# Attention, two MoE layers: where the loads, poolings and scatters of batches 4 to 7 stand in a hand-written order

## The chip, the cores and the metric
The kernel runs on one core of a Trainium2 chip. The core has five engines that work in parallel, each through its own instructions in program order: PE (matmul), DVE (VectorE), ACT (ScalarE), POOL (GpSimd) and SP, which here only issues DMAs. ACT and POOL issue DMAs too. The metric is the time of one execution in microseconds, on the device; the changed kernel is timed against this one.

## The reference
Three layers follow each other, in float32. Attention has 8 batches, 8 heads, 576 tokens and a head size of 64; keys and values are first averaged over groups of 8 tokens, so that each head has 72 of them.

```
k_p = k.reshape(B, H, 72, 8, D).mean(axis=3)          # v_p alike
attn = softmax(q @ k_p.T / sqrt(D));  x = attn @ v_p    # x: 4608 tokens x 512
e = argmax(x @ w_gate + modality_bias[modality_id])     # layer 1: one of 8 experts per token
x = gate_w * (relu(x @ w1[e]) @ w2[e])
noisy = x @ g + log1p(exp(x @ n)) * noise               # layer 2: the best two of 8 experts
out = sum over the two: weight * (relu(x @ w1[e]) @ w2[e])
```

## The kernel before, in words
Attention is cut into 36 steps of 128 tokens, t = 0 to 35; batch b begins at step first[b] = 0, 4, 9, 13, 18, 22, 27, 31. After it come 37 tiles of layer 1 and 76 of layer 2, in which PE multiplies without a pause. No planner is at work: the order of each engine's instructions is the order in which the program writes them, so an instruction that waits holds everything behind it on its own engine, and nothing else. A DMA that SP issues waits in SP's queue in the same way.

A step t of attention does, in this order: the transposes of the weights of t (PE, L798) and their copies out of PSUM (ACT, L799); the scores of step t + 3 for four heads (PE, L771) and their maxima (DVE, L779); the exponentials of t + 2 (ACT, L787); the store of x of step t - 1 to memory (a DMA on ACT's queue, L828); av(t), which multiplies by the pooled values (PE, L817) and writes the tile xr (DVE, L820 to L822), of which there are four buffers; the scores of the other four heads; and then the jobs of step t, a list that at_step fills before the loop begins. Jobs of one step run in the order in which they were added.

The jobs are: load_k, load_q, load_v (1152 KB each, SP's queue, two buffers each, so the load for batch b waits until batch b - 2 has been read); pool_k(b), the sum over 8 keys, on POOL (L707 to L709, L717); pool_v(b, pr) in four quarters, of which 0 and 1 are one DVE instruction each (L726) and 2 and 3 three POOL instructions each (L729 to L731); place_v(b), which copies the four quarters into place on ACT (L736); prep_v(b, hb), eight matmuls on PE (L742 to L745) and one copy on ACT (L746), of which each batch has two. The scores of step first[b] need pool_k(b) and the load of q, av of first[b] needs both prep_v(b).

The gate of layer 1 comes in five groups of 9, 9, 7, 6 and 5 steps (GO, GS). For the first four, gate_a and gate_b (small DVE instructions, L841 to L885, and matmuls L864) run in the two steps after a group is whole; then gate_c scatters one step's entries of the group into a list in memory, by an indirect DMA that POOL issues (L187); the first of a group also makes three copies (L893 to L895). After the third group (SNAP), pick_first reads the first expert's number into registers of SP and POOL, snapshot1 reads a part of the list back once all its scatters have landed (SP, L940), and SP's queue goes on with the weights of that expert (L227), which ACT and DVE split at steps 33 to 35 (L231, L232).

Fills: init_dram(2) and (1) fill two lists in memory from a tile that DVE writes (L147), init_dram(0) sets the tile zt to zero on POOL (L143) and fills the last rows of x with it; zero(out) fills the output from zt, one block a step from step 28.

In the order before, jobs of batch b stand at fixed distances from first[b]: pool_k at first[b] - 7, the quarters of pool_v at 6 to 4 steps before, place_v 3, prep_v 2 and 1 before; the loads of batch b + 1 at first[b] - 5, - 4 and - 3. The scatters of a group are spread over the steps behind its gate, one or two a step.

Of the kernel before, what the change touches and what calls it, by code (L numbers as in the profile page):

```python
# [8 lines left out]
F32 = mybir.dt.float32  # L9
# [10 lines left out]
P = 128  # L20
B, H, S, D = 8, 8, 576, 64
POOL, SP_ = 8, 72
N, DM, E, F = 4608, 512, 8, 1024
NT = N // P
BT = 9
GS = (9, 9, 7, 6, 5)
GO = (0, 9, 18, 25, 31, 36)
NG, GM, SNAP = 5, 9, 2
# [13 lines left out]
def kernel(ctx: ExitStack, tc: tile.TileContext, a: dict):  # L42
# [5 lines left out]
    V, A, G = nc.vector, nc.scalar, nc.gpsimd  # L48
# [18 lines left out]
    def bank(k):  # L67
        return psp.tile([P, 512], F32, name=f"bank{k}")
# [57 lines left out]
    zt = const.tile([P, DM // 2], F32, name="zt")  # L126
# [10 lines left out]
    def zero(dst, t):  # L137
        nc.sync.dma_start(dst[t * P:(t + 1) * P, :].rearrange("p (a d) -> p a d", a=2),
                          zt.unsqueeze(1).to_broadcast([P, 2, DM // 2]))

    def init_dram(k):
        if k == 0:
            G.memset(zt, 0.0)  # L143
            zero(x_d, N // P)
        else:
            dst = (l2_d, l1_d)[k - 1]
            V.tensor_copy(lsti, padi[:, 2 - k:3 - k, :].to_broadcast([P, LC, 4]))  # L147
            nc.sync.dma_start(dst.rearrange("(p c) k -> p (c k)", p=P), lst.rearrange("p c k -> p (c k)"))
# [535 lines left out]
    with actx:  # L684
        wk = actx.enter_context(tc.tile_pool(name="wk", bufs=2))
# [63 lines left out]
        def segs(t):  # L749
            g, l = divmod(t, BT)  # L750
            if l < 4:
                return [(2 * g, l * P, 0, P)]
            if l == 4:
                return [(2 * g, 512, 0, 64), (2 * g + 1, 0, 64, 64)]
            return [(2 * g + 1, l * P - S, 0, P)]
# [48 lines left out]
        def av(t):  # L804
            g = max(n for n in range(NG) if GO[n] <= t)
            l = t - GO[g]
            if l == 0:
                lgs[g] = gp.tile([P, GM, E], F32, name="lg")
            et = ets.pop(t)
            rs = wk.tile([P, 2, 4], F32, name="rs")  # L810
            xr = wk.tile([P, 2, D + E, 4], F32, name="xr", bufs=4)
            for hb in range(2):
                p = bank(5 + hb)[:, 0:4 * VW].rearrange("p (w h) -> p w h", h=4)
                for b, tok, r0, n in segs(t):
                    for c in range(3):
                        r = 96 if c == 1 else 97
                        nc.tensor.matmul(p[r0:r0 + n, :, c:c + 2],  # L817
                                         et[hb][0:r, c, r0:r0 + n], vb[b % NB][0:r, 3 * hb + c],
                                         start=(c == 0), stop=(c == 2), skip_group_check=True)
                V.reciprocal(rs[:, hb], p[:, VW - 1, :])  # L820
                V.tensor_tensor(xr[:, hb], p[:, 0:D + E, :], rs[:, hb].unsqueeze(1).to_broadcast([P, D + E, 4]), op=OP.mult)
            V.tensor_reduce(lgs[g][:, l, :], xr[:, :, D:D + E, :].rearrange("p a e h -> p e a h"), axis=mybir.AxisListType.XY, op=OP.add)  # L822
            xrs[t] = xr
# [74 lines left out]
        first = [BT * (b // 2) + 4 * (b % 2) for b in range(B)] + [99, 99]  # L898
# [5 lines left out]
        def at_step(t, f, *args):  # L904
            jobs.setdefault(t, []).append((f, args))

        for b in range(1, B):
            at_step(max(first[b] - 7, -1), pool_k, b, G)
            for pr, k in enumerate((5, 4, 6, 5)):
                at_step(max(first[b] - k, -1), pool_v, b, pr)  # L910
            at_step(first[b] - 3, place_v, b)
            at_step(first[b] - 2, prep_v, b, 0)
            at_step(first[b] - 1, prep_v, b, 1)
            if b + 1 < B:
                at_step(max(first[b] - 5, -1), issue, load_k, b + 1)
                at_step(first[b] - 4, issue, load_v, b + 1)
                at_step(first[b] - 3, issue, load_q, b + 1)
        at_step(0, init_small)
        at_step(14, split_gate)
        for t in range(6):  # L920
            at_step(28 + t, zero, out_d, t)
        for t, k in ((3, 2), (16, 0), (20, 1)):
            at_step(t, init_dram, k)
        for g in range(NG - 1):
            t = GO[g + 1]
            at_step(t, gate_a, g)
            at_step(t + 1, gate_b, g)
            for k in range(GS[g]):
                at_step(t + 2 + (k // 2 if g == SNAP else (k + 1) // 2 if g < SNAP else 1 + k // 3), gate_c, g, k)

        early = [Tile() for _ in range(K1)]
        pairs = [[Tile() for _ in range(4)] for _ in range(2)]
# [20 lines left out]
        def split_w1(i):  # L953
            split_pair(pairs[0][i], 2 * i, 0, V)

        at_step(GO[SNAP + 1] + 2, pick_first)
        at_step(GO[SNAP + 1] + 6, snapshot1)
        for i in range(K1):
            at_step(GO[SNAP + 1] + 7 + i if i < 2 else NT - 1, load_early, i)
# [5 lines left out]
        for h in range(2):  # L965
            r = slice(64 * h, 64 * h + 64)
# [21 lines left out]
        maxes(2, 1)  # L988
        prep_v(0, 1)
        av(0)  # L990
        for t in range(NT):
            if t:
                transp(t)
            if t == NT - 1:
                xT(early[0])
            for i in {34: (1, 2), 35: (3,)}.get(t, ()):
                split_w1(i)
            scores(t + 3, 0)
            maxes(t + 3, 0)
            expo(t + 2)  # L1000
            if t:
                store_x(t - 1)
                av(t)
            if t == 33:
                split_w1(0)
            scores(t + 3, 1)
            maxes(t + 3, 1)
            for n in range(-1 if t == 0 else t, t + 1):
                for f, args in jobs.pop(n, []):
                    f(*args)  # L1010
# [354 lines left out]
```

## Time and profile before

| what | value |
|---|---|
| time, median of 3 runs | 1483.0 us (1481.58 to 1483.82) |
| profiled execution, own time | 1486.63 us |
| its span, first to last instruction | 1484.9 us |
| PE busy | 1449.0 us, 98% |
| DVE, ACT busy | 1181.0 and 1200.2 us |
| POOL busy | 900.5 us, 61% |
| mean granted clock of PE | 0.996 |

The profile is of one execution, which is 3.6 us longer than the median of the timed ones. Busy times are those of instructions that compute; a DMA's issue by SP or ACT isn't one, an indirect DMA of POOL is, since POOL makes its descriptors. Attention with its gates takes up to about 175 us of the span. PE is the engine with the least idle time over the span.

### The profile page before, as it was taken

How to read it: one execution, taken by the hardware profiler on the slowest of the kernel's cores; microseconds unless marked ns; L12 is line 12 of the kernel's file. 1: busy time of each engine (PE TensorE's matmuls, PEld its weight loads, DVE VectorE, ACT ScalarE, POOL GpSimd, SP SyncE). 2: the span in 40 equal slices, each digit the busy share in tenths (PEclk: the TensorE clock that was granted, in tenths of full speed). 3: DMA queues.
4: the chain of work that ended last, by engine and by line, in shares of the span. 5: the costliest groups of instructions: out<-in, count | busy, mean ns of one | idle time of the engine just before them, and what ended most of it. 6: DMA issues, size and time to landing. Idle time of an engine off the chain costs nothing.

```text
span 1484.9 us, 31025 instructions
## 1 busy us (share of the span) xinstructions
PE 1449.0 (98%) x7485; PEld 1209.0 (81%) x7485; DVE 1181.0 (80%) x2995; ACT 1200.2 (81%) x3153; POOL 900.5 (61%) x1064
## 2 busy tenths in 40 slices
PE   7998899999999999999999999999999999999997
PEld 6988788888888888778888888888888888888886
DVE  6776767777777777779888888888888888888884
ACT  5766559888888888878888888888888888888883
POOL 7677568888888887665544544445445445444452
PEclk9999999999999999999999999999999999999999
DMA  8965555655555554444344344443443443434432
GB/s 320 339 222 181 187 137 146 161 161 147 142 140 140 142 142 135 132 101 107 89 107 93 88 106 93 100 98 89 107 93 86 107 93 92 102 92 104 94 88 45
DMA packets 136891, 191.10 MB, mean 129 GB/s; under 512 B 71376, under 2 KB 95184, under 8 KB 134032
## 3 DMA queue, kind: packets, MB, share of 16 engines
q1 hardware_dynamic: 102240, 129.67, 29.2%
q0 software_dynamic: 24688, 49.94, 17.2%
q10 hardware_dynamic: 9792, 9.44, 1.9%
q8 instruction: 80, 1.31, 0.4%
q14 instruction: 91, 0.75, 0.2%
HBM read 121.64 MB, written 52.82 MB: 117 GB/s over the span
## 4 chain that ended last, share of the span: by engine, by line
issue 36%; PE 33%; POOL 15%; DVE 4%; POOLq 4%; ACT 4%; DMA 2%; SPq 0%; another core or an unknown queue 0%; ACTq 0%; DVEq 0%
PE bank L294 8%; PE bank L296 8%; PE bank L295 8%; POOL out L453 8%; POOL w2l L223 5%; PE bank L817 3%; POOLq L174 3%; PE bank L332 2%; ACT xt L289 2%; PE bank L771 2%; PE bank L798 1%; DMA x_d<-xr 1%; POOLq L223 1%; DVE g2t L393 1%; POOL cur L244 1%
## 5 line engine op out<-in xcount | busy, mean ns | idle before, releaser
L312 DVE STREAM_TRANSPOSE ht<-h 32x256 f32<-32x256 f32 x1136 | 495.4, 436 | 95.9 <-ACT h L305 81.3
L289 ACT ACTIVATE xt<-xz 32x128 f32<-32x128 f32 x1728 | 531.4, 308 | 34.6 <-DVE xz L282 13.5
L294 PE MATMUL bank<-w1h,xh 128*128 (+1 forms) x904 | 357.3, 395 | 0.0
L295 PE MATMUL bank<-w1l,xh 128*128 (+1 forms) x904 | 354.6, 392 | 0.0
L296 PE MATMUL bank<-w1h,xl 128*128 (+1 forms) x904 | 353.7, 391 | 0.0
L296 PE MATMUL bank<-w2h,hl 128*128 (+1 forms) x896 | 351.7, 393 | 0.1
L295 PE MATMUL bank<-w2l,hh 128*128 (+1 forms) x896 | 351.4, 392 | 0.0
L294 PE MATMUL bank<-w2h,hh 128*128 (+1 forms) x896 | 350.6, 391 | 0.0
L223 POOL TENSOR_TENSOR w1l<-sg,w1h 128x512 f32 x109 | 140.7, 1291 | 237.5 <-ACT w1h L220 231.3
L453 POOL DMA_INDIRECT out<-yo,cur x76 | 121.1, 1593 | 163.4 <-ACT yo L450 155.9
L296 PEld LDWEIGHTS bank<-w2h,hl 128*128 128x128 f32 x896 | 168.3, 188 | 39.7 <-DVE hl L321 3.3
L296 PEld LDWEIGHTS bank<-w1h,xl 128*128 128x128 f32 x904 | 169.8, 188 | 36.8
L294 PEld LDWEIGHTS bank<-w1h,xh 128*128 128x128 f32 x904 | 169.7, 188 | 36.3
L295 PEld LDWEIGHTS bank<-w1l,xh 128*128 128x128 f32 x904 | 169.9, 188 | 35.2
L294 PEld LDWEIGHTS bank<-w2h,hh 128*128 128x128 f32 x896 | 168.3, 188 | 37.2
L295 PEld LDWEIGHTS bank<-w2l,hh 128*128 128x128 f32 x896 | 168.3, 188 | 36.4
L305 ACT ACTIVATE h<-bank 128x512 f32<-128x512 f32 x226 | 133.0, 589 | 68.5 <-PE bank L296 59.8
L223 POOL TENSOR_TENSOR w2l<-sg,w2h 128x512 f32 x109 | 141.5, 1298 | 14.3 <-ACT w2h L220 14.3
L250 POOL DMA_INDIRECT x<-x_d,cur x113 | 124.1, 1098 | 37.7 <-POOL cur L244 33.4
L320 ACT ACTIVATE hh<-ht 128x1024 fp32r<-128x1024 f32 x71 | 75.4, 1062 | 58.6 <-DVE ht L312 30.6
L278 DVE TENSOR_TENSOR xl<-xt,xh 128x512 fp32r<-128x512 f32 x108 | 77.2, 715 | 56.0 <-ACT xh L274 43.4
L187 POOL DMA_INDIRECT l_d<-le,dst x74 | 80.1, 1083 | 28.8 <-issue 12.3
(269 smaller groups left out, 1979.2 us busy)
## 6 DMA issues: line engine op xcount, KB each, us to landing
sg<-w SPq DMA_DIRECT2D x118, 512.0 KB
out<-zt SPq DMA_DIRECT2D x37, 256.0 KB
x_d<-yo SPq DMA_DIRECT2D x37, 256.0 KB
x_d<-xr ACTq DMA_DIRECT2D x36, 256.0 KB
kk<-kT SPq DMA_DIRECT2D x7, 1152.0 KB
q<-qT SPq DMA_DIRECT2D x7, 1152.0 KB
vv<-vT SPq DMA_DIRECT2D x7, 1152.0 KB
x_d<-zt SPq DMA_DIRECT2D x10, 256.0 KB
```

The source lines that it names most:

```text
L187: ins = G.indirect_dma_start(out=dram_t, out_offset=bass.IndirectOffsetOnAxis(ap=ix, axis=0), in_=src, in_offset=None, bounds_check=P * LC ...
L223: eng.tensor_tensor(l, u.sg[:, k, :], h.bitcast(F32), op=OP.subtract)
L250: G.indirect_dma_start(out=u.x, out_offset=None, in_=src[0:top, :], in_offset=off, bounds_check=top - 1, oob_is_err=True)
L278: V.tensor_tensor(u.xl, p, u.xh.bitcast(F32), op=OP.subtract)
L289: A.activation(u.xt[32 * q:32 * q + 32, :, 32 * i:32 * i + 32], zv[:, q], AF.Copy)
L294: nc.tensor.matmul(p, hs, rh, start=first, stop=False)
L295: nc.tensor.matmul(p, hs, rl, start=False, stop=False)
L296: nc.tensor.matmul(p, ls, rh, start=False, stop=last)
L305: A.activation(u.h[:, 512 * hf:512 * hf + 512], p, AF.Relu)
L312: V.transpose(out=t[32 * q:32 * q + 32, :, 32 * i:32 * i + 32], in_=hv[:, q])
L320: A.activation(u.hh, u.t, AF.Copy)
L453: G.indirect_dma_start(out=out_d, out_offset=bass.IndirectOffsetOnAxis(ap=u.ci[:, 2:3], axis=0), in_=u.yo, in_offset=None, bounds_check=N ...
```

## The change
The order of the jobs of batches 1 to 3 stays, except that the loads of k and v of batch 5 now stand at step 10, ahead of q of batch 4. For batches 4 to 7 steps are written out one by one:

| job | batch 4 | batch 5 | batch 6 | batch 7 |
|---|---|---|---|---|
| load k, before / after | 8 / 8 | 13 / 10 | 17 / 14 | 22 / 15 |
| load v | 9 / 9 | 14 / 10 | 18 / 15 | 23 / 18 |
| load q | 10 / 10 | 15 / 15 | 19 / 19 | 24 / 24 |
| pool_k | 11 / 12 | 15 / 14 | 20 / 16 | 24 / 21 |
| POOL's quarters of pool_v | 12, 13 / 12, 13 | 16, 17 / 15, 15 | 21, 22 / 17, 17 | 25, 26 / 22, 22 |
| DVE's quarters of pool_v | 13, 14 / 13, 14 | 17, 18 / 16, 17 | 22, 23 / 20, 21 | 26, 27 / 22, 23 |
| place_v | 15 / 15 | 19 / 19 | 24 / 22 | 28 / 24 |
| prep_v | 16, 17 / same | 20, 21 / same | 25, 26 / 23, 24 | 29, 30 / 27, 28 |

The scatters of the first two gates leave the steps 11 to 15 and 20 to 24: the first of each group stays at steps 11 and 20, the other eight stand together, four a step, at 18 and 19 and at 23 and 24. The fill of the second list moves from step 20 to 15, the memset of zt from step 16 to 5, split_gate from 14 to 13, pick_first from 27 to 28. xr gets seven buffers instead of four. No instruction is added or left out.

```diff
--- before.py
+++ after.py
@@ -140,7 +140,6 @@
 
     def init_dram(k):
         if k == 0:
-            G.memset(zt, 0.0)
             zero(x_d, N // P)
         else:
             dst = (l2_d, l1_d)[k - 1]
@@ -808,7 +807,7 @@
                 lgs[g] = gp.tile([P, GM, E], F32, name="lg")
             et = ets.pop(t)
             rs = wk.tile([P, 2, 4], F32, name="rs")
-            xr = wk.tile([P, 2, D + E, 4], F32, name="xr", bufs=4)
+            xr = wk.tile([P, 2, D + E, 4], F32, name="xr", bufs=7)
             for hb in range(2):
                 p = bank(5 + hb)[:, 0:4 * VW].rearrange("p (w h) -> p w h", h=4)
                 for b, tok, r0, n in segs(t):
@@ -904,29 +903,45 @@
         def at_step(t, f, *args):
             jobs.setdefault(t, []).append((f, args))
 
-        for b in range(1, B):
+        for b in range(1, 4):
             at_step(max(first[b] - 7, -1), pool_k, b, G)
             for pr, k in enumerate((5, 4, 6, 5)):
                 at_step(max(first[b] - k, -1), pool_v, b, pr)
             at_step(first[b] - 3, place_v, b)
             at_step(first[b] - 2, prep_v, b, 0)
             at_step(first[b] - 1, prep_v, b, 1)
-            if b + 1 < B:
-                at_step(max(first[b] - 5, -1), issue, load_k, b + 1)
-                at_step(first[b] - 4, issue, load_v, b + 1)
-                at_step(first[b] - 3, issue, load_q, b + 1)
+            at_step(max(first[b] - 5, -1), issue, load_k, b + 1)
+            at_step(first[b] - 4, issue, load_v, b + 1)
+            if b == 3:
+                at_step(10, issue, load_k, 5)
+                at_step(10, issue, load_v, 5)
+            at_step(first[b] - 3, issue, load_q, b + 1)
         at_step(0, init_small)
-        at_step(14, split_gate)
+        at_step(5, G.memset, zt, 0.0)
+        at_step(11, gate_c, 0, 0)
+        at_step(20, gate_c, 1, 0)
+        for b, k, v, p, r in ((4, 12, (13, 14, 12, 13), 15, (16, 17)), (5, 14, (16, 17, 15, 15), 19, (20, 21)),
+                              (6, 16, (20, 21, 17, 17), 22, (23, 24)), (7, 21, (22, 23, 22, 22), 24, (27, 28))):
+            at_step(k, pool_k, b, G)
+            for pr in range(4):
+                at_step(v[pr], pool_v, b, pr)
+            at_step(p, place_v, b)
+            for hb in range(2):
+                at_step(r[hb], prep_v, b, hb)
+        for t, f, b in ((14, load_k, 6), (15, load_v, 6), (15, load_k, 7), (15, load_q, 5), (18, load_v, 7),
+                        (19, load_q, 6), (24, load_q, 7)):
+            at_step(t, issue, f, b)
+        at_step(13, split_gate)
         for t in range(6):
             at_step(28 + t, zero, out_d, t)
-        for t, k in ((3, 2), (16, 0), (20, 1)):
+        for t, k in ((3, 2), (16, 0), (15, 1)):
             at_step(t, init_dram, k)
         for g in range(NG - 1):
             t = GO[g + 1]
             at_step(t, gate_a, g)
             at_step(t + 1, gate_b, g)
-            for k in range(GS[g]):
-                at_step(t + 2 + (k // 2 if g == SNAP else (k + 1) // 2 if g < SNAP else 1 + k // 3), gate_c, g, k)
+            for k in range(0 if g >= SNAP else 1, GS[g]):
+                at_step((18, 23)[g] + (k - 1) // 4 if g < SNAP else t + 2 + (k // 2 if g == SNAP else 1 + k // 3), gate_c, g, k)
 
         early = [Tile() for _ in range(K1)]
         pairs = [[Tile() for _ in range(4)] for _ in range(2)]
@@ -953,7 +968,7 @@
         def split_w1(i):
             split_pair(pairs[0][i], 2 * i, 0, V)
 
-        at_step(GO[SNAP + 1] + 2, pick_first)
+        at_step(GO[SNAP + 1] + 3, pick_first)
         at_step(GO[SNAP + 1] + 6, snapshot1)
         for i in range(K1):
             at_step(GO[SNAP + 1] + 7 + i if i < 2 else NT - 1, load_early, i)
```

## Rows read from the trace of the kernel before

**Rows 1.** Stretches: from:to, us, busy PE, PEld, DVE, ACT, POOL, clock, DMA, GB/s.
```profile
100.00:120.00 20.00, 17.16 (x130) 16.16 (x128) 15.20 (x35) 10.30 (x39) 16.87 (x21) 0.91 0.93 332
...
140.00:160.00 20.00, 16.81 (x135) 15.94 (x133) 9.85 (x34) 10.71 (x42) 10.69 (x23) 0.91 0.67 219
```

**Rows 2.** Timeline of PE: start us, duration us, instruction, [idle before <- releaser].
```profile
62.65 0.38 PE L864 MATMUL bank<-goh,tri_bf 128*128 128x72 bf16 x9 [1.04 <-DVE goh L850]
...
78.44 0.82 PE L798 MATMUL bank<-ident_sb,e 128*96 128x128 f32 x6
...
81.67 0.82 PE L798 MATMUL bank<-ident_sb,e 128*96 128x128 f32 x6
...
85.98 0.82 PE L798 MATMUL bank<-ident_sb,e 128*96 128x128 f32 x6
...
105.21 2.10 PE L817 MATMUL bank<-vb,et 97*128 97x146 f32 x12 [2.11 <-DVE rs L820]
...
116.94 0.82 PE L798 MATMUL bank<-ident_sb,e 128*96 128x128 f32 x6
...
121.57 0.82 PE L798 MATMUL bank<-ident_sb,e 128*96 128x128 f32 x6
...
147.13 3.07 PE L817 MATMUL bank<-vb,et 97*128 97x146 f32 x12 [3.10 <-ACT et L799]
```

**Rows 3.** Timeline of DVE, steps 9 and 19.
```profile
58.11 0.46 DVE L821 TENSOR_TENSOR xr<-bank,rs 128x288 f32<-128x288 f32 x1 [1.17 <-DMA x_d<-xr]
...
99.82 2.60 DVE L181 TENSOR_SCALAR rb<-gqi 128x9 int32<-128x9 int32 x1
```

**Rows 4.** Timeline of POOL, steps 6 to 24.
```profile
45.99 2.63 POOL L707 TENSOR_TENSOR pool<-kk 128x1152 f32<-128x1152 f32 x1 [6.52 <-DMA kk<-kT]
...
53.06 0.80 POOL L729 TENSOR_TENSOR pool<-vv 128x288 f32<-128x288 f32 x1
...
56.48 2.63 POOL L707 TENSOR_TENSOR pool<-kk 128x1152 f32<-128x1152 f32 x1
...
67.39 1.20 POOL L187 DMA_INDIRECT l_d<-gle,dst  x1 [3.34 <-issue]
...
77.47 0.25 POOL L162 CAST wg_sb<-lt_t 128x64 bf16<-128x64 f32 x1
...
79.21 1.00 POOL L187 DMA_INDIRECT l_d<-gle,dst  x1 [0.42 <-issue]
...
99.76 2.62 POOL L707 TENSOR_TENSOR pool<-kk 128x1152 f32<-128x1152 f32 x1 [4.96 <-DMA kk<-kT]
...
106.83 0.20 POOL L893 COPY gle<-idx_sb 128x9 int32<-128x9 int32 x1
...
108.72 0.81 POOL L729 TENSOR_TENSOR pool<-vv 128x288 f32<-128x288 f32 x1
...
115.24 0.99 POOL L187 DMA_INDIRECT l_d<-gle,dst  x1 [0.41 <-issue]
...
120.07 2.64 POOL L707 TENSOR_TENSOR pool<-kk 128x1152 f32<-128x1152 f32 x1
```

**Rows 5.** Timeline of the SP queue, steps 18 to 32.
```profile
93.80 0.60 SPq L86 DMA_DIRECT2D kk<-kT  x1
...
138.34 2.60 SPq L138 DMA_DIRECT2D out<-zt  x4
...
146.04 0.36 SPq L940 DMA_DIRECT2D lst<-l_d  x1
...
147.63 17.57 SPq L227 DMA_DIRECT2D sg<-w  x4
```

**Rows 6.** Timeline of ACT, steps 24 to 33.
```profile
121.62 0.91 ACT L736 ACTIVATE vp<-vk 64x288 f32<-64x288 f32 x2
...
146.16 0.55 ACT L746 ACTIVATE vb<-bank 96x432 f32<-96x432 f32 x1 [4.38 <-remote]
...
162.06 1.09 ACT L231 ACTIVATE w1h<-sg 128x1024 fp32r<-128x1024 f32 x1
```

## The prediction

> **What bounds the kernel now.** I read the page first: PE is busy 98% of the span, so only time in which PE stands still can be won, and the change touches only the attention stage, steps 0 to 35, up to about 175 us. Then the stretches of 20 us: in two of them, 100 to 120 and 140 to 160, PE is busy 17.16 and 16.81 us and its granted clock is 0.91, a stretch at the lower level [rows 1]. Then the timelines of PE, DVE, POOL, the SP queue and ACT, engine by engine, to find what ended each pause. A step is told by its six transposes (L798): 78.44 to 81.67 us is a step without prep_v (3.23 us), 81.67 to 85.98 one with it (4.31 us), so one prep_v costs PE 1.08 us [rows 2]. Inside the steps PE works without a gap; it is the bound, and everything else counts only where it makes PE late. PE is late in four places: 1.04 us at 62.65 (gate of step 10), 2.11 us at 105.21, a step of 4.63 us instead of 3.23 from 116.94 to 121.57, and 3.10 us at 147.13 [rows 2].
>
> **The change, part by part.**
>
> *Seven buffers for xr.* At step 9 DVE waits 1.17 us for a store of x five steps old before it may write xr again [rows 3]; PE then misses the gate's one-hot by 1.04 us [rows 2]. With seven buffers the store has three steps more. Saved: 1.0 us (between 0, if another load delays the stores again, and 1.2).
>
> *The pause at step 20.* POOL's pool_k of batch 6 had waited 4.96 us for its load and starts at 99.76 [rows 4]; the load was issued at 93.80 [rows 5], behind the fill of x's last rows, which waits for the memset of zt, an instruction of POOL's queue at step 16. DVE's gate instruction L181, on nine numbers a partition, starts 0.06 us later and takes 2.60 us, about as long as POOL's 2.62 [rows 3, 4]. So PE idles 2.11 us [rows 2], and the clock then costs (1 - 0.91) x 20 = 1.8 us [rows 1]: 3.9 us together. After the change the memset stands at step 5, the load at step 14, and pool_k of batch 6 is over before this gate. Saved: 3.9 us (0 if POOL stands in another long instruction there).
>
> The Trainium skill (SBUF — State Buffer, "Who interferes with whom") says that DVE and GpSimd hold a shared port pair exclusively for a whole instruction, DVE instructions with two SBUF inputs included; the 2.60 beside 2.62 agrees. The rule speaks against the new order too: POOL is then in poolings without a break, and at the gate of step 19 it is in pool_v of batch 6, whose longest instruction takes 0.80 us, so three of the gate's instructions could lose 2.4 us by it instead of nothing. In the sum this changes nothing, because POOL's queue decides a few steps later; it would take that much from rival C.
>
> *The step of 4.63 us.* 1.4 us too long, beside four scatters in a row from 115.24 [rows 4]. Gone (1.4) or kept (0): the next part makes either alike.
>
> *POOL's queue.* Here I expect the new limit. POOL works in order and the whole queue counts. Prices from start to start: pool_k 53.06 - 45.99 = 7.07 us; the two POOL quarters of a pool_v 56.48 - 53.06 = 3.42; split_gate 79.21 - 77.47, less the lead of a scatter, about 1.4; four scatters in a row 120.07 - 115.24 = 4.83, so 1.21 each; the three copies with the first scatter of a group 108.72 - 106.83 = 1.89 [rows 4]. Before, pool_k of batch 4 (step 11) stands ahead of the first scatter and runs at 56.48. After, the first scatter (step 11) stands ahead of pool_k of batch 4 (step 12). It needs the gate of step 10, so it starts at 67.39 - 1.04 = 66.35 as before [rows 4], and POOL stands idle from 56.5 until then. From there nothing waits any more, and the queue is one block: scatter 1.2; batches 4, 5 and 6 three times (7.07 + 3.42) = 31.5; split_gate 1.4; eight scatters 9.7 with 0.4 of lead; copies and scatter 1.9; batch 7 10.5. That sum is 56.6, so pool_v of batch 7 is done at 66.35 + 56.6 = 123.0 us.
>
> *place_v of batch 7 at step 24.* This is ACT's, four steps earlier than before, and everything of ACT behind it waits: the copies of the transposes of step 25 and so PE's av of step 25. In the run of before ACT reaches the jobs of step 24 at 121.62 [rows 6]. With the gains it would be there at 121.62 - 1.0 - 3.9 - 1.4 = 115.3, plus 2.2 for the two prep_v of batch 6, which now lie ahead of this point: 117.5. It waits until 123.0, 5.5 us. As long a pause as this was followed by a stretch at the lower clock both times before (2.11 and 3.10 us idle, [rows 1, 2]); I add 1.8. So up to here: saved 6.3, lost 5.5 + 1.8 = 7.3, net +1.0 us. If the 1.4 us stay, the wait is 1.4 shorter and the net is the same; equally for the load of q of batch 5, now behind a load that waits for pool_k of batch 5 on the SP queue, and for DVE's fill of the list at step 15: whatever is late before step 24 only shortens this wait. The ends: -0.8 (no lower clock) and +2.
>
> *The stop at 142 to 147.* PE idles 3.10 us [rows 2] and loses 1.8 to the clock [rows 1], 4.9 us. ACT waits 4.38 us for a release that the profile puts down to "remote" [rows 6]; so the cause isn't shown. Beside it lie four fills of out, issued from 138.34 [rows 5], and the seven scatters of the third gate. After, pick_first stands at step 28, so that three fills come behind it instead of four, and all loads are done earlier; but the seven scatters follow directly on eight others. Ends: 0 (as before) and -4.9 (gone). I take the middle, -2.4, as nothing in the rows is nearer to either.
>
> *The tail.* POOL's queue after 123.0 has eight scatters and then the third gate's seven, four of them ahead of pick_first. pick_first one step (4.31 us) later makes the read of the list, at 146.04 before, about 3 to 4 us later, and the weights' loads behind it on the SP queue, at 147.63 [rows 5], with it. Their first user is ACT at 162.06, which did not wait [rows 6]; of 14.4 us some 6 remain even if the steps are 4.9 us early. Cost 0 to 2; I take 0.3.
>
> Everything after 180 us is PE-bound and shifts along. Sum: +1.0 - 2.4 + 0.3 = -1.1 us. Against the profiled execution (span 1484.9, 1486.63 with what lies around it) that is 1485.5; this execution lies 3.6 us above the median of the timed runs, 1483.0. The same difference gives 1481.9, so 1482 us. About 3 us, 0.2%, is what a measurement of this kernel can tell from no change.
>
> **The rivals.**
> A, the forecast: POOL's late block eats the gains, part of the later stop goes. 1482, own range 1480 to 1485.8. 0.45.
> B: as A, but the stop at 142 to 147 goes whole: +1.0 - 4.9 + 0.3 = -3.6, 1479.4. For it: its fills and scatters are spread otherwise. Against: a stop whose releaser the profile can't name may belong to that one execution, which was 3.6 us longer than the median; then the timed runs never had it, and nothing is won. 0.22.
> C: POOL isn't late at step 24, since the block is shorter than its sum or the steps are slower from other causes that the change also removes. Then 6.3 stand, and with 0 to 4.9 of the stop the time is 1472 to 1477, say 1474.5. Against it: each price is a distance between rows of the same queue, and nothing but the gate can start the block. 0.13.
> D, slower: scatters in a row hold the semaphores of the other engines. Four in a row stand beside 1.4 us lost, seven beside 4.9: 6.3 for eleven, 0.57 each. After the change fifteen follow each other from 123 us on, 8.6 us instead of 4.9, so +3.7 + 1.0 + 0.3 = +5.0 and 1488. It decides from 0.45 us for each. Against it: no load of attention lies beside them any more. 0.20.
>
> **How the numbers follow.** Faster by over 0.2%: B and C, 0.35. Within: A, 0.45. Slower: D, 0.20. The range takes in half of C and D's value: 1475.5 to 1488.
>
> **What would show it.** Right: in the changed kernel's POOL timeline no pause between the first scatter (about 66 us) and the end of pool_v of batch 7 (about 123 us); ACT's place_v of batch 7 ends an idle time of 4 to 6 us with POOL's vk named; PE idle as long, with a lower clock in that stretch; no DVE wait for a store of x; L181 of step 19 under 1 us. Wrong: place_v of batch 7 without a wait (then C); several pauses of PE beside the scatters of 123 to 148 us (then D); a pause at 105 us as before.

## The result: slower, and the profile after

The changed kernel takes 1491.4 us (median of 4 runs, 1490.57 to 1492.06) where the kernel before takes 1482.3 (4 runs): a ratio of 1.0061, 95% interval 1.0049 to 1.0074, some 9 us. The forecast was 1482, its range ended at 1488. In the profiled execution of the changed kernel (1491.15 us, span 1489.4) the line numbers of the attention part are one less than before.

First the stretches, as in [rows 1] (from:to, us, busy PE, PEld, DVE, ACT, POOL, clock, DMA, GB/s):

```profile
80.00:100.00 20.00, 20.00 (x174) 18.92 (x173) 16.86 (x54) 15.95 (x60) 18.34 (x22) 1.00 1.03 378
100.00:120.00 20.00, 13.86 (x97) 13.00 (x96) 9.03 (x25) 8.55 (x30) 16.82 (x18) 0.74 0.20 65
120.00:140.00 20.00, 15.83 (x128) 14.72 (x127) 10.18 (x35) 12.24 (x45) 10.58 (x17) 1.00 0.42 127
140.00:160.00 20.00, 17.75 (x154) 16.37 (x153) 13.04 (x55) 12.39 (x49) 6.82 (x7) 1.00 0.34 108
```

Most of the loss is in one stretch: from 100 to 120 PE is busy 13.86 us (17.16 before) and the clock is 0.74. PE stands still from 106.33 to 112.48; in that pause the granted clock falls from 2.4 to 1.2 GHz, and it stays there for a while (0.50 from 109 to 118 us). DVE and ACT are busy less than before as well (9.03 for 15.20 and 8.55 for 10.30); only POOL is as busy as before (16.82 for 16.87). Now PE, ACT and POOL in that stretch, in their timelines (start, duration, instruction, [idle before <- releaser]). PE:

```profile
104.77 0.41 PE L744 MATMUL bank<-rc,vp 128*96 128x146 f32 x2
105.02 0.82 PE L797 MATMUL bank<-ident_sb,e 128*96 128x128 f32 x6
105.67 0.66 PE L770 MATMUL bank<-kb,q 128*128 128x144 f32 x4
112.48 1.30 PE L816 MATMUL bank<-vb,et 97*64 97x146 f32 x6 [6.14 <-ACT et L798]
```

ACT:

```profile
110.45 0.55 ACT L745 ACTIVATE vb<-bank 96x432 f32<-96x432 f32 x1 [6.53 <-remote]
111.94 0.49 ACT L798 ACTIVATE et<-bank 96x384 f32<-96x384 f32 x1 [0.93 <-remote]
113.35 0.49 ACT L798 ACTIVATE et<-bank 96x384 f32<-96x384 f32 x1 [0.93 <-remote]
...
115.37 0.91 ACT L735 ACTIVATE vp<-vk 64x288 f32<-64x288 f32 x2
```

POOL:

```profile
65.76 1.20 POOL L186 DMA_INDIRECT l_d<-gle,dst  x1 [9.58 <-issue]
66.98 2.65 POOL L706 TENSOR_TENSOR pool<-kk 128x1152 f32<-128x1152 f32 x1
...
100.34 1.06 POOL L186 DMA_INDIRECT l_d<-gle,dst  x1 [0.44 <-issue]
101.71 0.98 POOL L186 DMA_INDIRECT l_d<-gle,dst  x1 [0.30 <-issue]
...
109.40 0.97 POOL L186 DMA_INDIRECT l_d<-gle,dst  x1 [0.30 <-issue]
...
122.37 0.32 POOL L730 TENSOR_TENSOR vk<-pool 128x72 f32<-128x72 f32 x1
```

Read the first two together. PE's matmuls for vb (L744) end at 105.18 and its transposes (L797) at 105.84. ACT copies their results, needs nothing else, and starts on them at 110.45, 111.94 and 113.35, at steps of 1.4 us. So the work was done and the message that it was done came late. The trace holds the events of the semaphore that PE raises: they stand at 107.51, 110.43, 111.85, 113.27 and 113.33, although the last recorded matmul before them ended at 106.33. "Remote" is what the profile writes when it finds no instruction that ended near the event. DVE's own events are on time meanwhile (106.79 and 108.66, for instructions that ended at 106.78 and 108.65), so it is PE's messages that are late. Beside it POOL issues eight scatters in a row, 1.28 us apart, from 100.34 to 110.37. The same mark stood in [rows 6], ACT's 4.38 "remote" at 146.16, beside five scatters in a row; the prediction noted it and left its cause open.

Along the program, PE's transposes of a step compared in the two traces: after is 1.06 us early from step 11 on, 4.91 early at step 22, 3.54 late at step 23 (8.45 lost in one step), 5.2 late at step 24, 9.08 at step 30, 3.14 at step 31 (here before has its own pause), 5.28 at step 35, 7.6 at 185 us and 8.67 at 284 us. From there to 600 us nothing changes. Between 600 and 658 us it wins 3.95 back: the kernel before waits there five times, 3.5 us in all, for x3t (the transposed loads in front of layer 2), the changed one once, 0.2 us. The spans differ by 4.53 us and the medians by 9.1, because the profiled execution of before lay 4.3 us above the median of its four runs and that of the changed kernel 0.2 below its own.

### The profile page after: what moved, and what is told of

The parts are those of the page before. It is cut to its first block, busy times and chain, and to the rows that moved or that the text cites. A ratio compares the mean times of both kernels' runs of the same rounds, so it can differ in the third digit from the quotient of the medians.

```text
span 1489.4 us, 31022 instructions
## 1 busy us (share of the span) xinstructions
PE 1449.5 (97%) x7485; PEld 1209.3 (81%) x7485; DVE 1176.3 (79%) x2995; ACT 1201.3 (81%) x3153; POOL 913.6 (61%) x1064
## 4 chain that ended last, share of the span: by engine, by line
PE 40%; issue 36%; POOL 15%; POOLq 4%; DMA 1%; DVE 1%; ACT 1%; another core or an unknown queue 1%; SPq 0%; ACTq 0%; DVEq 0%
PE bank L293 10%; PE bank L295 9%; PE bank L294 9%; POOL out L452 8%; POOL w2l L222 5%; PE bank L816 4%; POOLq L173 3%; PE bank L770 2%; PE bank L331 2%; PE bank L797 1%; POOLq L222 1%; PE bank L370 1%; POOL cur L243 1%; POOL x L249 1%
## 5 line engine op out<-in xcount | busy, mean ns | idle before, releaser
L186 POOL DMA_INDIRECT l_d<-le,dst x74 | 89.0, 1202 | 26.1 <-issue 12.3
```

What stands on the lines that cost most here:

```text
L186: ins = G.indirect_dma_start(out=dram_t, out_offset=bass.IndirectOffsetOnAxis(ap=ix, axis=0), in_=src, in_offset=None, bounds_check=P * LC ...
```

## The experiments

Two theories. S: while POOL issues indirect DMAs in a row, PE's signals come late, and PE stops. Q, the forecast's: POOL's late queue makes ACT's place_v of batch 7 wait. Each kernel was timed in turns with the kernel before on the same chip. Chips differ, and these runs lie on five of them (e1 to e4; e5 to e8; e9 to e12; e13 to e15; e16 to e18). So ratios are compared, not times, and ratios from two chips only where their intervals lie apart. The ratio is taken from the single runs and isn't the quotient of the two medians beside it. The traces of the variants are held against the first trace of before; since that execution lay some 4 us above the median, a variant can be level with it in the trace and still lose some 4 us in the timed runs.

| run | ratio to before, 95% interval | median / before, us |
|---|---|---|
| e1_scatters | 1.0043 (1.0026 to 1.0059) | 1488.4 / 1482.8 |
| e2_spread | 1.0046 (1.0029 to 1.0063) | 1489.5 / 1482.8 |
| e3_place | 1.0074 (1.0055 to 1.0093) | 1492.9 / 1482.8 |
| e4_min | 1.0029 (1.0015 to 1.0044) | 1486.7 / 1482.8 |
| e5_six | 1.0034 (1.0022 to 1.0046) | 1485.4 / 1480.7 |
| e6_queue | 1.0020 (1.0009 to 1.0031) | 1483.8 / 1480.7 |
| e7_gap | 1.0032 (1.0020 to 1.0045) | 1486.1 / 1480.7 |
| e8_pairs | 0.9975 (0.9965 to 0.9985) | 1478.1 / 1480.7 |
| e9_tail | 1.0031 (1.0020 to 1.0043) | 1484.9 / 1480.5 |
| e10_gathers | 1.0034 (1.0021 to 1.0047) | 1484.3 / 1480.5 |
| e11_plain | 1.0028 (1.0016 to 1.0040) | 1484.5 / 1480.5 |
| e12_third | 0.9986 (0.9975 to 0.9997) | 1477.9 / 1480.5 |
| e13_before | one run | 1475.6 / 1474.6 |
| e14_after | 1.0039 (1.0024 to 1.0053) | 1480.1 / 1474.6 |
| e15_pairs | 1.0049 (1.0034 to 1.0064) | 1481.9 / 1474.6 |
| e16_six | 1.0046 (1.0028 to 1.0064) | 1487.0 / 1480.9 |
| e17_place | 1.0066 (1.0053 to 1.0079) | 1490.3 / 1480.9 |
| e18_pairs | 0.9976 (0.9967 to 0.9984) | 1476.6 / 1480.9 |

**e1: only the scatters.** The kernel before, with the scatters of the first two gates at the steps of the change.

```diff
-for k in range(GS[g]):
-    at_step(t + 2 + (... (k + 1) // 2 if g < SNAP ...), gate_c, g, k)
+for k in range(0 if g >= SNAP else 1, GS[g]):
+    at_step((18, 23)[g] + (k - 1) // 4 if g < SNAP else ..., gate_c, g, k)
```

> The kernel before, in which only the scatters of the first two gates are regrouped as in the change: the first of each at steps 11 and 20, the others four a step at 18, 19 and 23, 24. Theory S (scatters in a row hold back PE's signals): PE stops beside the rows of eight as it does in the changed kernel, 6 to 10 us slower than before, about 1488 to 1492. Theory Q (the late queue of POOL ahead of place_v is what costs): here place_v of batch 7 stands at step 28 and POOL's poolings come earlier than before, so no loss, 1480 to 1484, and no stop beside the scatters.

ACT and then PE in the timeline of e1, beside its eight scatters (the first starts at 84.30, the last at 93.30):

```profile
95.94 0.55 ACT L746 ACTIVATE vb<-bank 96x432 f32<-96x432 f32 x1 [6.93 <-remote]
```

```profile
90.11 0.82 PE L798 MATMUL bank<-ident_sb,e 128*96 128x128 f32 x6
...
96.91 3.29 PE L817 MATMUL bank<-vb,et 97*128 97x146 f32 x12 [5.49 <-ACT et L799]
```

One part of the change alone makes the same stop: PE loses 7.4 us in one step and is 7.3 late at step 19. It also makes most of the loss, a ratio of 1.0043 where the change has 1.0061. S holds; with place_v at step 28 as before, Q can't be the cause of this stop.

**e2: everything but the scatters.** The change, with the scatters at the steps of before.

> The changed kernel, in which only the scatters go back to the steps they had before, one or two a step (11 to 15 and 20 to 24); loads, poolings, fills and the seven buffers stay. S: the stops beside the rows of eight go; the time falls by 6 to 10 us, to 1481 to 1486, though POOL's poolings now wait for the scatters between them and place_v of batch 6 or 7 may wait 2 to 5 us. Q: POOL's queue ahead of place_v is longer by all the scatters that now stand between the poolings, so it gets no faster: 1490 to 1495.

The stop is gone, and the time isn't shown to be better: 1.0046, with an interval that overlaps that of the change. S had expected 1481 to 1486, so it missed here. Signals are at most 0.7 us late beside the six scatters in a row from 125.9 on, which POOL's late queue pushes together, and 1.1 beside the four behind them. In its place come 2.9 us of PE waiting for q of batch 5 (issued behind the load of kk for batch 7) and two waits of ACT for pooled values, 1.94 and 3.01. So Q's losses are there as soon as S's are not.

**e3: place_v of batch 7 at step 26 instead of 24.**

> The changed kernel with place_v of batch 7 at step 26 instead of 24, nothing else. S: the stop of the first row of eight has already made the steps late, so that place_v waits for under 2 us of POOL anyway; no difference beyond 2 us, 1489 to 1492. Q: the wait of ACT goes, 4 us or more faster, 1485 to 1487.

No gain, as S expected: ACT's "remote" of 6.51 at 110.20 is there, and another of 6.09 at 131.71.

**e4: seven buffers for xr and the early zt, nothing else.**

```diff
-            G.memset(zt, 0.0)
...
-            xr = wk.tile([P, 2, D + E, 4], F32, name="xr", bufs=4)
+            xr = wk.tile([P, 2, D + E, 4], F32, name="xr", bufs=7)
...
+        at_step(5, G.memset, zt, 0.0)
```

> The kernel before with only seven buffers for xr and the memset of zt at step 5. By the trace of before the pause of 1.0 us at step 10 and that of 3.9 us at step 20 (half clock included) can go, as batch 6's load no longer stands behind the memset: 1477 to 1481. S and Q expect the same here, since neither scatters nor place_v move. If the pause at step 20 isn't the load's but only moves to another instruction, 1481 to 1484.

The two savings are real in their own rows (the wait at step 9 is gone and PE's pause of 1.04 is 0.22; the load of batch 6 is 15 us earlier), but the pause at step 20 only moved. DVE in the timeline of e4, the gate of the second group, then POOL:

```profile
94.15 2.14 DVE L840 TENSOR_TENSOR lg<-lg,biasg 128x72 f32<-128x72 f32 x1
96.33 0.23 DVE L842 TENSOR_REDUCE gm<-lg 128x9 f32<-128x72 f32 x1
96.59 1.18 DVE L844 TENSOR_TENSOR geq<-lg,gm 128x72 f32<-128x72 f32 x1
97.80 0.83 DVE L845 TENSOR_TENSOR geq<-geq,cst_sb 128x72 f32<-128x72 f32 x1
```

```profile
93.57 2.63 POOL L706 TENSOR_TENSOR pool<-kk 128x1152 f32<-128x1152 f32 x1
```

POOL's pool_k of batch 6 has instructions of 2.63, 1.40 and 0.79 us beside these; in the changed kernel's first gate, at 59.41, where POOL stands idle, the same L840, L844 and L845 take 0.22, 0.23 and 0.23. PE then idles 2.84 at 99.22 instead of 2.11. That agrees with the rule of the Trainium skill weighed in the prediction (SBUF — State Buffer, "Who interferes with whom"): the instructions that read two tiles of SBUF wait for POOL's, the reduce between them (0.23) doesn't. The expected gain was missed: the ratio is 1.0029, the twelve runs spread from 1480.9 to 1493.1, and the trace is of the fastest. Why the kernel is slower than before is not shown.

**e5, e10, e11, e16: six DMAs in a row on POOL at step 5**, where POOL otherwise waits, added to the kernel before: scatters (e5, and once more on another chip e16), indirect gathers of 32 bytes a row, where a scatter moves 16, that nothing reads (e10), plain DMAs of the scatters' size (e11). The listing shows the three loop bodies, of which each run has one:

```diff
+        for k in range(6):
+            at_step(5, scatter, extra, l2_d, idx[:, k:k + 1], cst[:, 4 * k:4 * k + 4])   # e5, e16
+            at_step(5, gather, k)                # e10: G.indirect_dma_start from noise
+            at_step(5, G.dma_start, l2_d[k * P:k * P + P, :], cst[:, 4 * k:4 * k + 4])   # e11
```

> The kernel before with six more scatters, in a row, at step 5, of rows that nobody reads, into the second list ahead of its fill (POOL stands idle there for 6.5 us, about 39.5 to 46 us; the six take 7.7). Nothing else changes. S: PE's signals come late beside them and PE stops at some place between 43 and 50 us, 2 to 6 us in all, 1485 to 1489. Q, or any theory in which only the order of the poolings counts: POOL's next pooling starts 1 to 2 us later and is needed 10 us after, so no loss, 1482 to 1484.

> The kernel before with six indirect gathers of 32 bytes a token in a row on POOL at step 5, where e5_six had six scatters; nothing reads what they fetch. If any indirect DMA in a row on POOL holds PE's signals back: a stop of 3 to 5 us at steps 6 to 8 and +3 to +5 us (ratio 1.002 to 1.0035). If only scattered writes do: no stop there, ratio within 0.999 to 1.001. If it is only that POOL is busy and comes late to its poolings, the same time as e5_six without late signals of PE.

> The kernel before with six plain DMAs in a row on POOL at step 5 (128 rows of 16 bytes each, to the same rows of memory that e5_six scatters to, and in the same size). If writing many small pieces is what holds PE's signals back: a stop of 3 to 5 us at steps 6 to 8 and +3 to +5 us. If it takes the making of indirect descriptors on POOL: no stop, ratio within 0.999 to 1.001.

> The kernel before with six extra scatters in a row at step 5, once more. If late signals of PE go with the chip or the execution: either a stop of 3 to 4.5 at steps 6 to 8 with late signals beside it and a ratio of 1.002 to 1.0045, or neither, with PE's steps 6 to 11 as in the kernel before to 0.3 us and a ratio of 0.999 to 1.0015. If the row of scatters stops PE everywhere: the stop is there in any case.

PE in the timeline of e5 (the scatters stand from 39.74 to 47.39), then ACT in that of e10 (the gathers from 39.5 to 47.4):

```profile
46.33 0.82 PE L798 MATMUL bank<-ident_sb,e 128*96 128x128 f32 x6
46.98 0.66 PE L771 MATMUL bank<-kb,q 128*128 128x144 f32 x4
49.81 2.35 PE L817 MATMUL bank<-vb,et 97*128 97x146 f32 x12 [2.17 <-DVE rs L820]
```

```profile
48.53 0.86 ACT L799 ACTIVATE et<-bank 96x384 f32<-96x384 f32 x2 [2.38 <-remote]
```

Against their own step 6, PE is 4.6 us late at step 8 in e5 and in e16 and 2.5 in e10, each with late signals at 48.3 to 49.0; in e11 it is on time to 0.1 us and no signal is late there. So indirect DMAs in either direction do it, and plain ones of the same size don't. One difference is left: the six plain DMAs hold POOL for 3.5 us (39.17 to 42.68), the indirect ones for 7.7, so a plain row as long as theirs wasn't seen. The times don't follow as neatly. e11 was expected at 0.999 to 1.001 and is about as slow as the others (1.0028, +4.0 us); its trace doesn't show where: from 180 us on it is ahead of the first trace of before. In e5 and e16 3.5 and 3.0 of the 4.6 us are won back at the pauses of steps 10 and 20. How much of these four ratios is the stop stays open.

**e6 and e7: parts of a repair.** e6 is e2 with pool_k of batch 4 at step 10, q of batch 5 at step 14 and place_v of batch 7 at step 26; e7 is the change with a small memset (288 columns) between the scatters of the first two gates, which stand 1.49 apart instead of 1.28.

> The run with the scatters spread as before, its POOL queue put right: pool_k of batch 4 at step 10, ahead of the first scatter, instead of 12; the load of q of batch 5 at step 14, ahead of v of batch 6 and k of batch 7; place_v of batch 7 at step 26. If what that run lost was POOL's late queue and the late q (waits of 2.9 us for q and 5.0 us for the pooled values), 5 to 7 us faster than it, 1482 to 1485; if it lost to stops beside scatters, no more than 1 us faster, 1488 to 1490.

> The changed kernel with one small memset of POOL's own scratch (288 numbers a partition, some 0.3 us) between any two scatters of the first two gates, 14 in all. POOL's queue gets 5 us longer. S, if it is the unbroken row that counts: the stops shrink, 1483 to 1488. S, if it is the number of scatters within some 10 us: as the changed kernel, 1490 to 1493. Q: slower by about the added queue, 1494 to 1497.

e6 takes Q's waits away and is left with late signals (1.3 and 1.1 us) beside six scatters in a row at 119.5 and four later: 1.0020, where e2 has 1.0046, with intervals that just overlap. Its 1483.8 us are in the range expected if e2 lost to Q's waits (1482 to 1485), though on another chip. e7 still has signals 1.3 to 2.7 late, and ACT waits "remote" 2.51 at 112.49 and 4.15 at 136.70: a gap of 0.2 us makes the stop smaller and doesn't take it away. Its ratio, 1.0032, is below that of the change though POOL has more to do, as S expected and Q didn't. And with the stop smaller, Q's wait shows: ACT waits 2.93 for the pooled values at 124.09, and PE 3.84.

**e8, e18: pairs.** e4, with no more than two scatters together up to the third gate: batches 4 to 7 as before, the scatters that stood in fours spread by twos between the poolings, the third gate's parted by a memset of 1.1 us, pool_k of batch 6 behind the gate, and the second list's fill at step 15. Of the edit:

```diff
+            if g == SNAP and t in (2, 4, 6):
+                G.memset(rp.tile([P, 4, 4 * SP_], F32, name="pool1"), 0.0)
...
+        at_step(20, gate_c, 1, 0)          # ahead of pool_k(6)
...
+        at_step(18, gate_c, 0, 5); at_step(18, gate_c, 0, 6)
+        at_step(18, split_gate)
+        at_step(18, gate_c, 0, 7); at_step(18, gate_c, 0, 8)
```

> The run with seven buffers and the early memset, and no more than two scatters in a row anywhere up to the third gate: scatters in pairs between poolings, the third gate's pairs apart by a memset of 1.1 us, pool_k of batch 6 behind the first scatter of the second gate, so that it can't run beside that gate, the second list's fill at step 15. S: the stops go, and with them the spread of the times; 1476 to 1480. If the stops have another cause, the gates' pauses alone go: 1480 to 1484, and the times spread as before.

> The faster variant with pairs (seven buffers, zt early, batches as before, scatters in pairs), once more. Where signals come late: ratio 0.9965 to 0.9985 again, since the stops of before are taken away. Where they don't: only xr (1.0) and the pause at step 20 (0.8 to 2.1) are to be won, ratio 0.998 to 0.9995.

This one is faster than the kernel before, by 0.25% on two chips, and the change is slower than that kernel. In e18 the eleven times lie within 2.1 us, as expected; in e8 the twelve still spread by 7.5. Stretches of e18, columns as above:

```profile
100.00:120.00 20.00, 19.79 (x166) 19.03 (x165) 14.28 (x45) 15.09 (x57) 16.61 (x17) 1.00 0.79 289
120.00:140.00 20.00, 18.64 (x159) 17.31 (x158) 17.10 (x62) 13.64 (x50) 16.87 (x23) 1.00 0.34 110
```

PE is busy 19.79 of 20 us where the changed kernel has 13.86 and before 17.16, at the full clock; PE is 9.3 us ahead of before at step 31.

**e9, e12: the rows of the other gates.** e9 is e8 with the fourth and fifth gate's scatters parted into pairs too, by eight small memsets each time, 1.3 us together; e12 is the kernel before with only the third gate's parted.

> The faster variant with pairs (e8), and the eleven scatters of the fourth and fifth gate in pairs too, parted by eight small memsets of about 1 us together. If rows of scatters hold PE back there as well, PE's pause before the gate's matmuls at the end of attention (2.8 in e8, waiting for ACT's h) goes, and the time is 1 to 2 us below e8: ratio to before 0.996 to 0.997. If that pause has another cause (the load of the weights, the gathers of the first tiles), the time is e8's, ratio 0.9975, or up to 1 us above it, since the scatters end 4 us later.

> The kernel before with a memset of about 1.1 us on POOL ahead of every second scatter of the third gate, so that two stand together instead of five. If those five cause the pause of 3.10 us at 147.13 in the kernel before, it goes: PE idle under 1 us at step 30, and the time is 2 to 4.9 us lower where the timed runs had the pause (ratio 0.9967 to 0.9985). If the pause belongs to that one execution or to the fills of out: ratio 0.9995 to 1.001, since POOL reads the list 2 to 3 us later.

e12: the pause of [rows 2] at 147.13 is gone (0.14 us late at step 30, 4.7 early at step 31), and before gets 0.14% faster by three added instructions. The ratio expected was 0.9967 to 0.9985, so it is just missed. e9: the pause of 2.8 before L331 shrinks to 0.3, as S says, but the fifth gate's last scatter ends 5 us later than in e8 and the read of the list behind it as well. PE in the timeline of e9:

```profile
197.64 1.09 PE L267 MATMUL bank<-ident_sb,x 128*128 128x128 f32 x4 [6.01 <-DMA x<-x_d,cur]
```

So the last gate's row is on the path that sets the end, and a gap there costs more than it gives. The expectation was missed by some 7 us.

**e13 to e15: both kernels once more, and the change in pairs.** e13 and e14 are the kernels before and after, unchanged; e15 is the change with a memset of 1.1 us ahead of every second of the eight scatters, and of the third gate's.

> The kernel before, unchanged, for a second trace. If the waits for x3t at 598 to 658 us (five or six of about 0.6) belonged to the first execution alone: they are missing here or sum to under 1 us, and the span is 1479 to 1481 instead of 1484.9. If they belong to the kernel: 3 to 4 us again. The pause beside the third gate's five scatters in a row (3.10 at 147.13) is here again if the row of scatters causes it; if it was an accident of that execution, it is under 1 us.

> The changed kernel, unchanged, for a second trace and on the same chip as the others: 8 to 10 us above before (ratio 1.0055 to 1.007). If the row of eight scatters causes the loss, PE stands still for 4 to 7 us beside the first eight (about 100 to 110 us) here too, and falls behind again beside the second eight. If that was an accident, the pause is elsewhere or under 2 us.

> The changed kernel with a memset of about 1.1 us ahead of every second of the eight scatters of the first and second gate and of the third gate's, so that no more than two stand together; place, order and number are the change's, and POOL gets 3.3 us more work for each gate. If standing in a row costs the time: no pause over 1 us beside the first eight, and 1482 to 1485 (3 us of it from place_v of batch 7, which then waits for POOL some 6 to 9 us late). If the number of scatters or their place costs it: as the change or slower, since POOL has 10 us more to do: 1491 to 1497.

On this chip no signal of PE is late (by over 0.5 us) in any of the three traces. The kernel before runs in 1474.6 instead of 1480 to 1483, its pause at 142 to 147 is missing (PE is 8.3 us ahead of the first trace at step 31), and rows of scatters stop nothing, neither the third gate's seven in e13 (133.6 to 142.3) nor the eight of e14 (99.87 to 109.87). Of the 8 to 10 us expected of e14 5.5 came. They are what the change costs where no signal is late, and here the forecast's own mechanism is seen. ACT, then PE, in the timeline of e14, then its stretch 120 to 140:

```profile
104.75 0.57 ACT L745 ACTIVATE vb<-bank 96x432 f32<-96x432 f32 x1 [1.30 <-PE bank L744]
...
122.19 0.89 ACT L735 ACTIVATE vp<-vk 64x288 f32<-64x288 f32 x2 [4.59 <-POOL vk L730]
```

```profile
123.65 3.29 PE L816 MATMUL bank<-vb,et 97*128 97x146 f32 x12 [5.51 <-ACT et L798]
126.73 1.17 PE L770 MATMUL bank<-kb,q 128*128 128x144 f32 x4
127.69 0.99 PE L797 MATMUL bank<-ident_sb,e 128*96 128x128 f32 x6
...
129.01 1.75 PE L816 MATMUL bank<-vb,et 97*128 97x146 f32 x12
130.60 0.65 PE L770 MATMUL bank<-kb,q 128*128 128x144 f32 x4
```

```profile
120.00:140.00 20.00, 16.35 (x124) 15.49 (x125) 11.04 (x45) 11.72 (x44) 14.06 (x20) 0.83 0.18 55
```

e15 agrees: the first gate's three memsets, 3.3 us more ahead of the poolings of batch 7, make ACT's wait 7.4 and PE's 8.3. The expected 3 us of loss for it were too few, since it was reckoned for a chip with late signals; and the change with pairs on a chip where signals are late was not measured. As to x3t, before waits for it here too, 2.1 us in four waits, between the two expectations. Every kernel has some of these waits, but their sum changes with the execution: 0.49 and 2.03 us in e3 and e17, 3.15 and 0.70 in e8 and e18, which are one kernel each.

**e17: e3 on another chip.**

> The changed kernel with place_v of batch 7 at step 26 instead of 24. If ACT's wait at step 24 is what the change itself costs (where no signal comes late): PE's pause of 5.5 at 123 us is gone, and so is the stretch at 0.83 clock behind it; 4 to 7 us less than the changed kernel, so a ratio to before of 0.999 to 1.0005. If signals come late here as in the first trace: no gain, ratio 1.005 to 1.009 as before.

Signals come late again (PE waits 6.11 at 112.14), and the later place_v gains nothing. The repair of Q was not measured where signals are on time.

## Why the prediction was wrong, point by point

*Seven buffers for xr*: right. 1.0 forecast, 1.06 found; DVE's wait of [rows 3] is gone.

*The pause at step 20*: right for the two first traces, 3.85 found of 3.9 (1.06 early at step 21, 4.91 at step 22). But the 3.9 are one execution's: in e13 PE pauses 0.83 there and no lower clock follows, so that e14 wins 0.9; there it is L183, which reads two tiles where L181 reads one, that takes 2.54 beside POOL's 2.62. In the changed kernel L180 of that gate takes 0.16 us, where [rows 3] has 2.60. Beside pool_v the gate's L844 and L845 take 0.45 and 0.47, some 0.5 us more and not the 2.4 that three instructions could have lost. e4 shows what the saving hangs on: POOL must not stand in pool_k beside the gate.

*POOL's queue*: right. The first scatter starts at 65.76 (66.35 forecast), pool_v of batch 7 is done at 122.69 (123.0), with no pause between.

*place_v of batch 7*: not what happened in the timed comparison. ACT came to it at 127.91, 5.2 us after POOL was done, and didn't wait. On the chip without late signals the step is right as it was written: a wait of 4.59 (5.5 forecast) and PE idle 5.51. The clock is at its lower level from about 121 to 128 us, and what that costs is read from PE's rows: av and the four scores behind it take 3.08 and 0.96 from start to start, and 1.59 and 0.49 in the next step at full clock. So it costs 2.0 us, near the 1.8 of the forecast. The sum misses there too, +5.5 against -1.1: of the savings only 2.0 are found in e14 against e13 (1.1 for xr, 0.9 at step 20), the 1.4 beside four scatters and the stop at 142 to 147 aren't in e13 to be saved, and PE waits 2.23 at 203.67 for a tile of x, in the tail that was put at 0.3.

*The step that failed* is the sentence that whatever is late before step 24 only shortens this wait, and with it the line that the 1.4 us beside four scatters are gone or kept alike. The sum so has no term for the first eight scatters in a row. Cover holds only up to the length of the wait, 5.5 us, and these scatters, right there, cost 8.45 in one step, lower clock included. The row of four with the 1.4 us before was the small case of it: in the first trace of before PE's events of 119.52 and 120.93 are 1.3 and 1.2 late beside it, and in e13, where none is, that step takes 3.22 instead of 4.63.

*Rival D* named the mechanism and put it in the wrong place and at half the price: from 123 us on, 0.57 each, 3.7 us more. The first eight, at 100 to 110 us, cost 8.45 / 8 = 1.06 each, and the second eight, from 123.10 to 133.06, at or just behind which PE stops 1.76, 0.44 and 1.73 us, came on top. The fifteen that were to follow each other didn't: the third gate's stand apart, four from 142.65 and three from 152.42. Its reason against, that no load lies beside them, was no reason: the DMA share from 100 to 120 was 0.20.

*The stop at 142 to 147*: gone in the changed kernel (1.10 us are left at 149.71), as in B, and worth the 5.9 us regained at step 31; but 5.5 had been lost between steps 23 and 30. The doubt that it belongs to one execution was half right: e13 doesn't have it; e1, e4, e5, e10, e11 and e16 do; e12 shows that the row of five makes it, on a chip where signals come late.

*The tail*: 0.3 taken, about 3.4 found (5.28 late at step 35, 8.67 at 284 us). The list was read at 158.84 instead of 146.04, and PE waits 2.85 at 185.63, with late signals beside the fourth gate's six scatters in a row (0.25 at the same place before). Whether that wait makes the 3.4 is not shown, since before had paused 2.82 at 175.78, beside its own six.

*Everything after 180 us shifts along*: wrong by 4 us in the two first traces, the waits for x3t. As these change from one execution to the next, no effect of the change is shown there.

## What to carry to other kernels

Look at a group of indirect DMAs not only for the time that it takes on its own engine: where a wait ends "remote" although its producer was done microseconds ago, see what GpSimd (POOL here) is issuing beside it. Put other work between such DMAs (about 1 us of it did here, 0.2 us didn't) so that no more than two stand together, unless their end is itself on the path. And when a cost is said to be covered by a later wait, compare its upper bound with the length of that wait.

## What the runs showed of the hardware

Beside four or more indirect DMAs in a row on POOL, PE's semaphore events came up to 7 us after the work, about one every 1.4 us; gathers did it too, plain DMAs in a shorter row didn't. On one of six sets of runs it was absent, with up to eight in a row, and that chip ran the kernel before 6 to 8 us faster. The traces differ in one more thing: e13 to e15 hold 916 to 919 events of PE's semaphore for the 920 or 921 instructions on record that raise it, the other seventeen 862 to 885, so records of events are missing where signals come late. What the chips differ in, and whether the profiler, which records every timed run, has a part in it, stays open.
